# RWKV-5 attention into a mixture of four experts: bf16 transposes of scaled keys, a state update without its own keys, and a new order of the start

## The chip, the cores and the metric

One core of a Trainium2 chip runs the kernel. The metric is the device time of one execution in microseconds; less is better. Before the change three runs gave a median of 408.93 us (405.3 to 409.14).

## The reference

For each of 4 batches and 8 heads, attention walks over 768 positions with a state of 48 x 48; its result, 3072 rows of 384, goes through four experts, whose outputs are weighted per row and added.

```python
for t in range(S):
    cur = np.einsum('bhd,bhe->bhde', u[None] * kt, vt)
    y[:, :, t] = np.einsum('bhd,bhde->bhe', rt, state + cur)
    state = w[None, :, :, None] * state + np.einsum('bhd,bhe->bhde', kt, vt)
...
p = domain_probs / (domain_probs.sum(-1, keepdims=True) + 1e-09)
for e in range(E):
    h = np.maximum(x @ w1[e], 0.0)
    out += p[:, e:e + 1] * (h @ w2[e])
```

Shapes: r, k, v (4, 8, 768, 48), w and u (8, 48), w1 (4, 384, 1024), w2 (4, 1024, 384), all float32.

## The kernel before

The sequence is cut into 6 pieces of 128 positions. A chunk is one piece of one batch, all 8 heads; chunk ci is batch ci % 4, piece ci // 4, so there are 24, and four chunks in a row (a group) are one piece of all four batches. The state passes from chunk ci to ci + 4.

Attention of a chunk is a row of steps. `load` (L70 to L76) fetches R, K and V, 192 KB each, on SP's queue, into six buffers each. `pre` (L172 to L185) works on POOL: Vb (V in bf16), ruk = R * K * U, Kh (keys scaled for the state, in bf16, three buffers), dv; DVE reduces ruk to dcoef in between. `stR` and `stK` transpose R and K on PE in fp32, four transposes each for pairs of heads padded to 64, and DVE multiplies each result, 512 columns, with a table of decay powers into RsT and KsT. `stAt` makes the 8 products of keys and rows, masked by DVE into AtM. `stY` adds state and AtM products in psum, and DVE evicts them with dv into Ysb. `stS` makes the state matmuls St from Kh and Vb; POOL scales the old state by w^128 and DVE adds St. `stX` transposes Ysb, and DVE copies it to xTe. RT_ps, KT_ps and xT_ps share one psum buffer (tag tr), Y_ps and St_ps another (tag ys).

The experts: `l1` makes 128 rows of the hidden layer for all four chunks of a group (3 matmuls of 512 columns, evicted with Relu by ACT to hTs), `l2` the output of one chunk (8 matmuls of 384 columns), which DVE adds into oacc with the weight p_nat. Both use four psum buffers (tag mm).

The order on PE and POOL is that of the code; DVE, ACT and SP are ordered by the framework's scheduler, and every engine works in order. For the first four chunks attention steps and expert 0, chunk by chunk (L381 to L392), alternate. Then come 23 slots, one for each pair of expert and group from (expert 1, group 0) on. A slot is four times `l1`, `l1`, `l2` of the slot before; after each of these 12 parts a counter decides how many attention steps follow. Slots 0 and 1 take 12 steps each, the others 6:

```python
rate = 3 if si < 2 else 1.5
...
carry += rate / 3
while carry >= 1:
    carry -= 1
    f = next(steps, None)
```

The steps of a chunk stand in the order R(ci), Y(ci-1), K(ci), S(ci-1), At(ci), X(ci-1). Slot 3 is expert 0 of group 1 and needs xTe of chunk 7. From slot 18 on no attention is left.

Weights are cast to bf16 by DMAs on POOL's queue (`load_w1`, `load_w2`, 768 KB each): those of expert 0 at the start, the other six after attention steps 4, 9, 15 and 21 of the first four chunks (L374). At the start SP's queue also carries two DMAs of w (L83, single floats) and six of the weights p (L144, 16 bytes a piece).

Of the kernel before, what the change touches and what calls it, by code (L numbers as in the profile page):

```python
# [18 lines left out]
def kernel(  # L19
# [40 lines left out]


    RtB = [inputs.tile([128, H, P2], F32, name=f"Rt{i}") for i in range(NIN)]
    KtB = [inputs.tile([128, H, P2], F32, name=f"Kt{i}") for i in range(NIN)]
    KhB = [inputs.tile([128, H, P2], BF16, name=f"Kh{i}") for i in range(3)]
    for t in RtB + KtB + KhB:
        nc.vector.memset(t[:, :, D:P2], 0.0)

    Vts = {}

    def load(ci):  # L70
        b, c = ci % B, ci // B
# [75 lines left out]
    p_sum = consts.tile([128, TOTC, 1], F32)  # L147
    nc.vector.reduce_sum(p_sum, p_nat, axis=AX.X)
    nc.vector.tensor_scalar(p_sum, p_sum, scalar1=1e-9, scalar2=None, op0=ALU.add)
    p_rec = consts.tile([128, TOTC, 1], F32)  # L150
    nc.vector.reciprocal(p_rec, p_sum)
    nc.vector.tensor_mul(p_nat, p_nat, p_rec.to_broadcast((128, TOTC, E)))


    Sbd = [[inputs.tile([128, NP, 2 * D], BF16, name=f"S{b}_{i}") for i in range(2)]
           for b in range(B)]
    for b in range(B):
        for i in range(2):
            nc.gpsimd.memset(Sbd[b][i], 0.0)
# [160 lines left out]
    def att_steps(first, last):  # L320

        for ci in range(first, last + 1):
# [4 lines left out]
            if old:  # L327
                yield lambda ci=ci: stY(ci - 1)
# [98 lines left out]
```

## Time and profile before

| | us |
|---|---|
| median of three runs | 408.93 |
| the profiled execution | 405.69 |
| its span, first to last instruction | 403.6 |
| PE busy in the span | 326.0 |
| DVE, ACT, POOL busy | 168.0, 123.2, 124.7 |

The span is 2.1 us shorter than the profiled execution, which itself lies 0.8% below the median. Busy times of PE overlap and hold waiting inside a matmul, so stages are read by start times, not by sums of durations.

### The profile page before, as it was taken

To read this page: it belongs to the slowest core of one execution; us is meant where nothing else is said; L and a number is where in the kernel's file an instruction comes from. 1 tells how busy PE (TensorE), PEld (TensorE's weight loads), DVE (VectorE), ACT (ScalarE), POOL (GpSimd) and SP (SyncE) were. 2 spreads that over 40 slices of the span, in tenths; PEclk is the share of its full clock that TensorE was granted. 3 is DMA by queue.
4 is the path that set the end of the run, shared out by engine and by line. 5 is a ranking of instruction groups with operands and counts; after the bars stand their busy time and mean duration, and the time that the engine had idled before them with its cause. 6 is when DMAs were issued, how large, how long until landed. Compare 5 with 4: busy or idle time off the path is not lost.

```text
span 403.6 us, 5634 instructions
## 1 busy us (share of the span) xinstructions
PE 326.0 (81%) x2224; PEld 186.5 (46%) x2224; DVE 168.0 (42%) x328; ACT 123.2 (31%) x230; POOL 124.7 (31%) x176
## 2 busy tenths in 40 slices
PE   0156780868678979779798797799999999999996
PEld 0035650435444535445445454455555565555553
DVE  1057631554544443543435335436554444222223
ACT  1221330122133223233242232323333433444440
POOL 6148874753335044052251350531220000000000
PEclk9999997598999899998899898989999999999999
DMA  7999999972212322112321110110000100010002
GB/s 126 133 171 186 193 193 183 175 116 57 43 39 60 88 49 40 22 39 41 97 58 41 39 22 19 47 52 2 1 2 20 60 0 2 0 60 19 2 0 78
DMA packets 87993, 25.96 MB, mean 64 GB/s; under 512 B 79008, under 2 KB 86432, under 8 KB 87968
## 3 DMA queue, kind: packets, MB, share of 16 engines
q1 hardware_dynamic: 82208, 19.33, 26.5%
q0 software_dynamic: 5760, 6.29, 9.1%
q8 instruction: 17, 0.28, 0.3%
q14 instruction: 8, 0.07, 0.0%
HBM read 27.18 MB, written 4.72 MB: 79 GB/s over the span
## 4 chain that ended last, share of the span: by engine, by line
PE 50%; POOL 22%; DVE 10%; issue 8%; DMA 7%; SPq 1%; ACT 1%; POOLq 0%; ACTq 0%
PE out_ps L293 22%; PE hT_ps L280 20%; POOL ruk L180 5%; POOL ruk L179 5%; DMA Vt<-in_v_dram 4%; DVE AtM L218 4%; POOL Kh L182 4%; POOL S L259 3%; POOL dv L184 3%; PE RT_ps L191 3%; PE KT_ps L201 2%; DMA wT<-in_w_dram 2%; POOL Vb L178 2%; DVE oacc L300 2%; SPq L83 1%
## 5 line engine op out<-in xcount | busy, mean ns | idle before, releaser
L284 ACT ACTIVATE hTs<-hT_ps 128x512 bf16<-128x512 f32 (+1 forms) x216 | 116.5, 549 | 254.7 <-PE hT_ps L280 252.7
L280 PE MATMUL hT_ps<-xTe,w_sb 128*128 128x512 bf16 (+1 forms) x648 | 155.4, 372 | 0.0
L293 PE MATMUL out_ps<-w_sb,hTs 128*128 128x384 bf16 x768 | 147.3, 338 | 0.0
L293 PEld LDWEIGHTS <-hTs 128*128 128x128 bf16 x768 | 75.9, 100 | 54.7 <-issue 5.5
L280 PEld LDWEIGHTS <-w_sb 128*128 128x128 bf16 x648 | 59.1, 102 | 46.7 <-issue 5.8
L300 DVE SCALAR_TENSOR_TENSOR oacc<-out_ps,p_nat,oacc 128x384 f32<-128x384 f32 x72 | 44.4, 617 | 77.4 <-PE out_ps L293 77.3
L182 POOL TENSOR_TENSOR Kh<-Kt,W_sd 128x384 bf16<-128x384 f32 x20 | 20.0, 998 | 116.1 <-PE St_ps L250 114.0
L191 PE MATMUL RT_ps<-ident_f,Rt 128*128 128x128 f32 x96 | 17.7, 313 | 46.2 <-DVE xTe L268 33.5
L183 DVE TENSOR_REDUCE dcoef<-ruk 128x8 f32<-128x384 f32 x24 | 13.2, 551 | 65.3 <-POOL ruk L180 65.3
L191 PEld LDWEIGHTS RT_ps<-ident_f,Rt 128*128 128x128 f32 x96 | 11.8, 156 | 55.6 <-DVE xTe L268 42.3
L218 DVE TENSOR_TENSOR AtM<-At_ps,mask 128x512 bf16<-128x512 f32 x48 | 30.9, 683 | 3.6 <-PE At_ps L212 3.5
L184 POOL TENSOR_TENSOR dv<-Vt,dcoef 128x384 f32<-128x384 f32 x24 | 19.9, 830 | 35.0 <-DVE Ysb L240 28.7
L201 PE MATMUL KT_ps<-ident_f,Kt 128*128 128x128 f32 x96 | 16.6, 301 | 12.7 <-DVE RsT L195 12.6
L298 DVE TENSOR_SCALAR oacc<-out_ps,p_nat 128x384 f32<-128x384 f32 x24 | 14.8, 617 | 24.7 <-PE out_ps L293 24.7
L180 POOL TENSOR_TENSOR ruk<-ruk,U_sd 128x384 f32<-128x384 f32 x24 | 23.8, 994 | 1.9
L179 POOL TENSOR_TENSOR ruk<-Rt,Kt 128x384 f32<-128x384 f32 x24 | 24.0, 999 | 0.0
L195 DVE TENSOR_TENSOR RsT<-RT_ps,W1T 128x512 bf16<-128x512 f32 x24 | 16.6, 690 | 16.2 <-PE RT_ps L191 16.2
L178 POOL CAST Vb<-Vt 128x384 bf16<-128x384 f32 x24 | 12.1, 506 | 25.9 <-DMA Vt<-in_v_dram 18.7
L201 PEld LDWEIGHTS KT_ps<-ident_f,Kt 128*128 128x128 f32 x96 | 12.6, 153 | 15.7 <-DVE RsT L195 14.2
L240 DVE TENSOR_TENSOR Ysb<-Y_ps,dv 128x384 bf16<-128x384 f32 x24 | 13.3, 556 | 13.1 <-PE Y_ps L236 12.8
L236 PE MATMUL Y_ps<-Vb,AtM 128*128 128x48 bf16 x192 | 10.1, 193 | 10.4 <-POOL dv L184 9.6
L205 DVE TENSOR_TENSOR KsT<-KT_ps,W2T 128x512 bf16<-128x512 f32 x24 | 16.4, 684 | 3.6 <-PE KT_ps L201 3.6
(48 smaller groups left out, 128.7 us busy)
## 6 DMA issues: line engine op xcount, KB each, us to landing
w_sb<-in_moe_w_dram POOLq DMA_DIRECT2D x8, 768.0 KB, 12.9
Rt<-in_r_dram SPq DMA_DIRECT2D x24, 192.0 KB, 4.2
Kt<-in_k_dram SPq DMA_DIRECT2D x24, 192.0 KB, 3.9
Vt<-in_v_dram SPq DMA_DIRECT2D x24, 192.0 KB, 4.6
out_dram<-oacc SPq DMA_DIRECT2D x24, 192.0 KB, 1.8
logw_bc<-in_w_dram SPq DMA_DIRECT2D x1, 192.0 KB, 4.5
U_sd<-in_u_dram SPq DMA_DIRECT2D x1, 192.0 KB, 5.9
p_nat<-in_moe_domain_probs_dram SPq DMA_DIRECT2D x6, 8.0 KB, 2.2
```

The source lines that it names most:

```text
L178: nc.gpsimd.tensor_copy(Vb, Vt)
L179: nc.gpsimd.tensor_mul(ruk, Rt[:, :, 0:D], Kt[:, :, 0:D])
L180: nc.gpsimd.tensor_mul(ruk, ruk, U_sd)
L182: nc.gpsimd.tensor_mul(Kh[:, :, 0:D], Kt[:, :, 0:D], W3_sd)
L184: nc.gpsimd.tensor_mul(dv, Vt, dcoef.to_broadcast((128, H, D)))
L191: nc.tensor.transpose(ps[:, q, :], s["Rt"][:, 2 * q:2 * q + 2, :].rearrange("p a b -> p (a b)"), ident_f)
L201: nc.tensor.transpose(ps[:, q, :], s["Kt"][:, 2 * q:2 * q + 2, :].rearrange("p a b -> p (a b)"), ident_f)
L218: nc.vector.tensor_mul(s["AtM"][:, j], ps[:, j], mask[:, None, :].to_broadcast((128, NP, C)))
L280: nc.tensor.matmul(ps[:, 0:n, :].rearrange("p a b -> p (a b)"), w1_sb[:, e, db, fb * 128:(fb + 1) * 128], xTe[:, db, s0:s0 + n, :].rearran ...
L284: nc.scalar.activation(hTs[:, fb, s0:s0 + n, :], ps[:, 0:n, :], AF.Relu)
L293: nc.tensor.matmul(ps, hTs[:, fb, s, :], w2_sb[:, e, fb, :], start=(fb == 0), stop=(fb == NFB - 1))
L300: nc.vector.scalar_tensor_tensor(oaccs[ci], in0=ps, scalar=pe, in1=oaccs[ci], op0=ALU.mult, op1=ALU.add)
```

## The change

- R and K are scaled first, by DVE, with tables W1_sd (w^t) and W2_sd (w^-(t+1)), into one bf16 tile RK; four such tiles. `stRK` transposes both in bf16, 8 transposes into one psum tile of 1,024 columns, and ACT copies it to RKT. RsT, KsT and their two products go.
- Kh goes. The state matmuls take the keys in RK; DVE adds them to the old state into Tn, and POOL multiplies Tn with w^128 into the new state.
- The order of a chunk's steps is RK(ci), Y(ci-1), S(ci-1), At(ci), X(ci-1): five instead of six, 10 a slot in slots 0 and 1, then 5. `pre` runs one chunk ahead of its transposes (LEAD).
- In the start the four chunks run one after the other, each beside expert 0 of the chunk before (`fill`).
- w and p come as rows (wrow, prow) and are transposed by PE; w^128 is squared up on DVE; the two tables of powers cost two activations. Loads 0 and 1 stand ahead of these rows on SP's queue.
- The weights are issued after `pre` of chunks 0 and 2 to 7.

The core of the diff:

```diff
-    KhB = [inputs.tile([128, H, P2], BF16, name=f"Kh{i}") for i in range(3)]
...
-            nc.sync.dma_start(wT[j * P2:j * P2 + D, :],
-                              w.rearrange("(q j) d -> j d q", j=2)[j])
...
+    logw_bc = consts.tile([128, HD], F32)
+    nc.sync.dma_start(logw_bc, w.rearrange("h d -> (h d)")[None, :].to_broadcast((128, HD)))
+    load_w1(0)
+    load(0)
...
+    load(1)
+
+    wrow = consts.tile([NP, 2, P2], F32)
+    nc.vector.memset(wrow, 1.0)
+    nc.sync.dma_start(wrow[:, :, 0:D], w.rearrange("(q j) d -> q j d", j=2))
+    prow = consts.tile([TOTC, C, E], F32)
+    nc.sync.dma_start(prow, moe_domain_probs.rearrange("(n p) e -> n p e", p=C))
...
-    for c in range(NCH):
-        nc.sync.dma_start(
-            p_nat[:, c * B:(c + 1) * B, :],
-            moe_domain_probs.rearrange("(b c p) e -> c p b e", b=B, p=128)[c])
...
+    RKB = [consts.tile([128, 2, H, P2], BF16, name=f"RK{i}") for i in range(NRK)]
...
+        nc.tensor.transpose(ps, wrow.rearrange("q j d -> q (j d)"), ident_f[0:NP, 0:NP])
+        nc.vector.tensor_copy(wC, ps)
+        for _ in range(7):
+            nc.vector.tensor_mul(wC, wC, wC)
...
     def pre(ci):
+        nc.vector.tensor_mul(RK[:, 0, :, 0:D], Rt, W1_sd)
+        nc.vector.tensor_mul(RK[:, 1, :, 0:D], Kt, W2_sd)
...
-        nc.gpsimd.tensor_copy(Vb, Vt)
-        nc.gpsimd.tensor_mul(ruk, Rt[:, :, 0:D], Kt[:, :, 0:D])
-        nc.gpsimd.tensor_mul(ruk, ruk, U_sd)
-        if ci // B < NCH - 1:
-            nc.gpsimd.tensor_mul(Kh[:, :, 0:D], Kt[:, :, 0:D], W3_sd)
-        nc.vector.reduce_sum(dcoef, ruk, axis=AX.X)
+        nc.gpsimd.tensor_mul(ruk, Rt, Kt)
+        nc.gpsimd.tensor_mul(ruk, ruk, U_sd)
+        nc.vector.reduce_sum(dcoef, ruk, axis=AX.X)
+        nc.gpsimd.tensor_copy(Vb, Vt)
         nc.gpsimd.tensor_mul(dv, Vt, dcoef.to_broadcast((128, H, D)))
...
+    def stRK(ci):
         s = st[ci]
+        ps = psum.tile([128, 2, NP, C], BF16, tag="tr", bufs=1, name="RKT_ps")
+        for i in range(2):
+            for q in range(NP):
+                nc.tensor.transpose(ps[:, i, q, :],
+                                    s["RK"][:, i, 2 * q:2 * q + 2, :].rearrange("p a b -> p (a b)"),
+                                    ident)
+        s["RKT"] = work.tile([128, 2, NP, C], BF16, tag="RKT", bufs=3, name="RKT")
+        nc.scalar.copy(s["RKT"], ps)
...
-                             s["Kh"][:, 2 * q:2 * q + 2, :].rearrange("p a b -> p (a b)"),
+                             s["RK"][:, 1, 2 * q:2 * q + 2, :].rearrange("p a b -> p (a b)"),
...
-                nc.gpsimd.tensor_mul(S_new[pr, :, cl], S_now[pr, :, cl],
-                                     wC[pr, :, None].to_broadcast((P2, NP, D)))
-                nc.vector.tensor_add(S_new[pr, :, cl], S_new[pr, :, cl], ps[pr, :, cl])
+                nc.vector.tensor_add(Tn[pr], S_now[pr, :, cl], ps[pr, :, cl])
+                nc.gpsimd.tensor_mul(S_new[pr, :, cl], Tn[pr], wCb)
...
+    after = {0: [lambda: load_w2(0)], 2: [lambda: load_w1(1)], 3: [lambda: load_w2(1)],
+             4: [lambda: load_w1(2)], 5: [lambda: load_w2(2)],
+             6: [lambda: load_w1(3)], 7: [lambda: load_w2(3)]}
...
+                if new:
+                    yield lambda ci=ci: (pre_upto(ci + LEAD), stRK(ci))
+                if old:
+                    yield lambda ci=ci: stY(ci - 1)
+                    yield lambda ci=ci: stS(ci - 1)
+                if new:
+                    yield lambda ci=ci: stAt(ci)
+                if old:
+                    yield lambda ci=ci: stX(ci - 1)
...
+            per = (10 if si < 2 else 5) / 12
```

What the change moves on the engines, at two places.

POOL, before, around the state of chunk 8; the names are those of `pre` and `stS`:

```order
L259 TENSOR_TENSOR S_1_177<-S_0_176,wC 64x4x48 x2
L178 CAST Vb<-Vt 128x384
L179 TENSOR_TENSOR ruk<-Rt_77,Kt_83 128x384
L180 TENSOR_TENSOR ruk<-ruk,U_sd 128x384
L182 TENSOR_TENSOR Kh_86<-Kt_83,W_sd 128x8x48
L184 TENSOR_TENSOR dv<-Vt,dcoef 128x384
```

POOL, now, around the state of chunk 8:

```order
L247 TENSOR_TENSOR S_1_126<-Tn,wC 64x4x48 x2
L173 TENSOR_TENSOR ruk<-Rt,Kt 128x384
L174 TENSOR_TENSOR ruk<-ruk,U_sd 128x384
L176 CAST Vb<-Vt 128x384
L177 TENSOR_TENSOR dv<-Vt,dcoef 128x384
```

Kh is gone, ruk follows directly on the state, Vb has moved behind it, and the state reads Tn, which DVE writes.

DVE, before, in a slot of the middle; S is the sum of state and St_ps:

```order
L261 TENSOR_TENSOR S_0_182<-S_0_182,St_ps 64x4x48 x2
L300 SCALAR_TENSOR_TENSOR oacc<-out_ps,p_nat,oacc 128x384
L183 TENSOR_REDUCE dcoef<-ruk 128x8
L218 TENSOR_TENSOR AtM<-At_ps,mask 128x512 x2
L300 SCALAR_TENSOR_TENSOR oacc<-out_ps,p_nat,oacc 128x384
L268 COPY xTe<-xT_ps 128x3x128
L195 TENSOR_TENSOR RsT<-RT_ps,W1T 128x512
```

DVE, now, in a slot of the middle (the tiles RK_119 and RK_120 are two of the four RK tiles):

```order
L285 TENSOR_SCALAR oacc<-out_ps,p_nat 128x384
L246 TENSOR_TENSOR Tn<-S_1_130,St_ps 64x192 x2
L168 TENSOR_TENSOR RK_119<-Kt,W_sd 128x8x48
L175 TENSOR_REDUCE dcoef<-ruk 128x8
L287 SCALAR_TENSOR_TENSOR oacc<-out_ps,p_nat,oacc 128x384
L202 TENSOR_TENSOR AtM<-At_ps,mask 128x512 x2
L254 COPY xTe<-xT_ps 128x3x128
```

dcoef still stands ahead of AtM and xTe; an oacc now stands directly ahead of the addition to the state, and the product of K between that and dcoef.

DVE, now, ahead of the eviction of Y of chunk 4 (Ysb); RK_117 takes chunk 8 here, RK_118 chunk 9:

```order
L168 TENSOR_TENSOR RK_120<-Kt,W_sd 128x8x48
L167 TENSOR_TENSOR RK_117<-Rt,W_sd 128x8x48
L285 TENSOR_SCALAR oacc<-out_ps,p_nat 128x384
L202 TENSOR_TENSOR AtM<-At_ps,mask 128x512 x2
L167 TENSOR_TENSOR RK_118<-Rt,W_sd 128x8x48
L224 TENSOR_TENSOR Ysb<-Y_ps,dv 128x384
```

Before, dcoef of chunk 7 stood in this place, and no instruction of DVE read a load.

## Rows read from the trace of the kernel before

**Rows 1.** Windows: stretch, us, busy PE PEld DVE ACT POOL, PEclk, DMA share, GB/s.

```profile
0.00:53.80 53.80, 24.12 (x244) 19.20 (x245) 23.24 (x63) 13.48 (x46) 33.33 (x55) 1.00 1.14 163
53.80:122.10 68.30, 45.56 (x322) 25.78 (x320) 29.01 (x55) 14.32 (x24) 32.90 (x44) 0.85 0.67 110
122.10:270.00 147.90, 126.86 (x833) 69.92 (x831) 63.50 (x119) 43.63 (x74) 48.63 (x66) 0.92 0.21 48
270.00:342.50 72.50, 72.18 (x519) 41.16 (x518) 36.53 (x66) 27.89 (x47) 9.86 (x12) 1.00 0.04 13
342.50:403.60 61.10, 57.29 (x316) 30.46 (x313) 15.72 (x26) 23.84 (x40) 0.00 (x0) 0.99 0.07 26
```

**Rows 2.** Waits, whole span: who waited for whom, us, times, longest.

```profile
POOL Kh L182 <- PE St_ps L250: 114.0, 13, 11.2
...
DVE dcoef L183 <- POOL ruk L180: 65.3, 20, 10.8
...
PE RT_ps L191 <- DVE xTe L268: 33.5, 13, 3.7
```

**Rows 3.** Timeline, one chunk: start us, us, engine line op [idle before].

```profile
204.83 0.33 PE L250 MATMUL St_ps<-Vb,Kh 128*128 128x96 bf16 x4
...
205.20 0.71 DVE L261 TENSOR_TENSOR S<-S,St_ps 64x192 bf16<-64x192 bf16 x2 [0.69 <-PE St_ps L250]
...
206.99 1.08 POOL L259 TENSOR_TENSOR S<-S,wC 64x192 bf16<-64x192 bf16 x2
...
208.60 1.00 POOL L179 TENSOR_TENSOR ruk<-Rt,Kt 128x384 f32<-128x384 f32 x1
...
210.70 0.55 DVE L183 TENSOR_REDUCE dcoef<-ruk 128x8 f32<-128x384 f32 x1 [3.59 <-POOL ruk L180]
211.17 1.28 DVE L218 TENSOR_TENSOR AtM<-At_ps,mask 128x512 bf16<-128x512 f32 x2
212.37 0.61 DVE L298 TENSOR_SCALAR oacc<-out_ps,p_nat 128x384 f32<-128x384 f32 x1
212.89 0.35 DVE L268 COPY xTe<-xT_ps 128x384 bf16<-128x384 bf16 x1
...
213.30 0.66 PE L191 MATMUL RT_ps<-ident_f,Rt 128*128 128x128 f32 x4 [2.35 <-DVE xTe L268]
```

**Rows 4.** Timeline of PE, one chunk after 280 us.

```profile
282.43 0.33 PE L250 MATMUL St_ps<-Vb,Kh 128*128 128x96 bf16 x4
...
286.93 0.33 PE L267 MATMUL xT_ps<-ident,Ysb 128*128 128x128 bf16 x3
287.10 1.46 PE L280 MATMUL hT_ps<-xTe,w_sb 128*128 128x512 bf16 x6
288.64 0.66 PE L191 MATMUL RT_ps<-ident_f,Rt 128*128 128x128 f32 x4
289.14 1.46 PE L293 MATMUL out_ps<-w_sb,hTs 128*128 128x384 bf16 x8
...
293.40 0.60 PE L201 MATMUL KT_ps<-ident_f,Kt 128*128 128x128 f32 x4
293.84 1.46 PE L280 MATMUL hT_ps<-xTe,w_sb 128*128 128x512 bf16 x6
295.14 0.33 PE L250 MATMUL St_ps<-Vb,Kh 128*128 128x96 bf16 x4
```

**Rows 5.** DMA queues, 33 to 66 us: packets, MB, share of 16 engines.

```profile
q0 software_dynamic: 4320, 4.72, 83.7%
q1 hardware_dynamic: 8220, 1.55, 37.5%
```

**Rows 6.** DMA queues, 66 to 80 us.

```profile
q1 hardware_dynamic: 13011, 2.46, 117.7%
```

**Rows 7.** Timeline of PE: the state matmuls of chunk 4.

```profile
75.53 0.48 PE L250 MATMUL St_ps<-Vb,Kh 128*128 128x96 bf16 x4 [1.13 <-DVE Ysb L240]
```

**Rows 8.** Lines by form: the 512-column eviction on ACT.

```profile
L284 ACT ACTIVATE hTs<-hT_ps 128x512 bf16<-128x512 f32 x184 | 109.7, 597 | 231.2 <-PE hT_ps L280 229.6
```

More of the change, by code (lines that the diff above doesn't have):

```diff
@@ L148 @@
[L148 to L159, printed above, removed]
+    W1_sd = consts.tile([128, H, D], F32)
@@ L184, in pre @@
         nc.gpsimd.tensor_mul(dv, Vt, dcoef.to_broadcast((128, H, D)))
[L185 to L187 removed]
+        st[ci] = dict(RK=RK, Vb=Vb, dv=dv)
+    def stRK(ci):
         s = st[ci]
[L189 to L195 removed]
@@ L207, in stAt @@
+        for i in range(2):
+            for q in range(NP):
[4 more added lines that the diff above has]
+        nc.scalar.copy(s["RKT"], ps)
     def stAt(ci):
@@ L312, in load_next, with pre_upto @@
             state["loaded"] += 1
-    def pre_next():
-        if state["pre"] < TOTC:
+    def pre_upto(n):
+        while state["pre"] < min(n, TOTC):
             pre(state["pre"])
+            for f in after.get(state["pre"], []):
+                f()
             state["pre"] += 1
             load_next()
-    def att_steps(first, last):
-        for ci in range(first, last + 1):
-            new, old = ci < last, ci > first
-            if new:
-                pre_next()
-                yield lambda ci=ci: stR(ci)
-            if old:
-                yield lambda ci=ci: stY(ci - 1)
-            if new:
-                yield lambda ci=ci: stK(ci)
-            if old:
-                yield lambda ci=ci: stS(ci - 1)
-            if new:
-                yield lambda ci=ci: stAt(ci)
-            if old:
-                yield lambda ci=ci: stX(ci - 1)
@@ L338, with run @@
[L338 to L367 removed]
+    def run(gen):
+        f = next(gen, None)
+        if f:
+            f()
@@ new lines, with fill, att_steps @@
+    with tc.manual_schedule(engines={ET.PE, ET.Pool}):
+        load_next()
+        load_next()
+        def fill(ci):
+            for half in range(2):
+                yield lambda half=half: [l1(0, 0, fb, ci, 1) for fb in range(4 * half, 4 * half + 4)]
+            yield lambda: l2(0, 0, ci)
+        prev = iter(())
+        for ci in range(SUB):
+            pre_upto(ci + 1)
+            stRK(ci)
+            if ci == 0:
+                late_consts()
+            run(prev)
+            stAt(ci)
+            run(prev)
+            stY(ci)
+            run(prev)
+            stS(ci)
+            stX(ci)
+            prev = fill(ci)
+        run(prev)
+        run(prev)
+        def att_steps(first, last):
+            for ci in range(first, last + 1):
+                new, old = ci < last, ci > first
+                if new:
[7 more added lines that the diff above has]
+                    yield lambda ci=ci: stX(ci - 1)
@@ L381 @@
                     while carry >= 1:
                         carry -= 1
-                        f = next(steps, None)
-                        if f:
-                            f()
-                if prev:
-                    prev.pop(0)()
-                carry += rate / 3
-                while carry >= 1:
-                    carry -= 1
-                    f = next(steps, None)
-                    if f:
-                        f()
-            prev = [lambda e=e, sc=sc, s=s: l2(e, sc, s) for s in range(SUB)]
@@ L395 @@
-        for f in prev:
+                        run(steps)
+            l2s = [lambda e=e, sc=sc, s=s: l2(e, sc, s) for s in range(SUB)]
+        for f in l2s:
             f()
```

186 lines of the change are left out of this document (70 added, 116 removed).

## The prediction

> **What bounds the kernel now.** I read the windows by stretch first [rows 1]. The last 61.1 us hold no attention; PE works there almost without a gap. From 270 us on PE is busy 72.18 of 72.50 us although attention still runs. Between 122.1 and 270 it is busy 126.9 of 147.9 us at a clock of 0.92, and before 122.1 it is busy 69.7 us in all. So there are two losses: the start, and a stall in each of the slots of the middle. No engine but PE is close to full in any stretch.
>
> The list of waits tells what the stall is [rows 2]: PE's transposes of R wait for DVE's copy of xTe, DVE's reduction dcoef waits for POOL's ruk, and POOL's Kh waits for PE's state matmuls. The timeline of one chunk shows them as one chain [rows 3]. PE starts the state matmuls St at 204.83; POOL, which has run ahead until its three Kh buffers were full, now does Kh, dv, two S and Vb before it reaches ruk at 208.60; dcoef starts at 210.70. DVE works in order, so AtM, oacc and xTe stand behind dcoef, and PE, which needs the psum buffer that xTe empties, gets to RT at 213.30, after 2.35 us without work. The chain from St to RT takes 8.47 us. A chunk without this stall shows what PE itself needs [rows 4]: 12.71 us from St to St, 0.25 of it a small wait before RT (the six matmuls from 287.10 take 1.29, as the first of the next run from 293.84 do with 1.30), so 12.46 of work. Slots 3 to 17 lie between 122.1 and 342.5 us: 220.4 / 15 = 14.7 us each.
>
> In the start the DMA sets the pace. While weights were in flight their queue moved 4.72 MB in 33 us and the loads' queue only 1.55 MB (47 GB/s) [rows 5]; alone, from 66 to 80 us, the loads' queue moved 2.46 MB (176 GB/s) [rows 6].
>
> **The change part by part.**
>
> Transposes. Each chunk loses 8 fp32 transposes: RT holds PE 289.14 - 288.64 = 0.50 us, KT 0.44 [rows 4]. It gains 8 in bf16. The nearest row is xT: 3 bf16 transposes of the same size in 287.10 - 286.93 = 0.17, so 8 take 0.45. Ends: nothing gained (0.94), or 0.45; I take 0.45, since operation, type and size are the same. Work per chunk becomes 12.46 - 0.49 = 11.97 us.
>
> Evictions. The two DVE products RsT and KsT go; one ACT copy of 1,024 columns comes. No row shows it; it lies between one and two evictions of 512 columns, 0.60 to 1.19 us [rows 8], and I take 1.1. Two of PE's steps lie between the transposes and At, and ACT was busy only 43.6 of 147.9 us [rows 1], so it costs nothing; uncovered it would be 1.1 us a chunk.
>
> RK on DVE. Two products with both operands in SBUF come to DVE. Bounds: below dcoef's 0.55 for as many elements, or POOL's 1.00 for the same product [rows 3]; I take 0.55. Together with the products that go, DVE's load stays as it is (63.5 of 147.9 us). But these products read loads: the one for R of chunk 9 stands ahead of the eviction of Y of chunk 4 in DVE's order, and DVE waits there for that load. This matters in the start.
>
> The chain. Kh and its wait go. POOL now multiplies the state after DVE's Tn, and goes straight on to ruk. From St: 0.37 to Tn; first add 0.36; two S 1.08; two ruk 2.10; dcoef to its successor 0.47; oacc 0.52; AtM 1.20; xTe 0.41 until PE may go [rows 3]. Sum 6.51, and 0.36 more because an oacc now stands directly ahead of Tn: 6.9 us. PE's own work from St to the next transposes was 288.64 - 282.43 - 0.25 = 5.96; the new rate of 5 steps a slot puts one more pair of l1 groups in it, 1.30 [rows 4], so 7.26. The chain is 0.4 us shorter than its cover. Bounds: no stall, or, if DVE's RK product and POOL's ones hold each other up, 0.55 longer, hence 0.15 plus the error of the sum. I take 0.2 us for each of the 11 slots from 3 to 13 that still have a state update: 2.2 us. If the cover is gone, RK is late next, and behind it on PE the whole l2 and l1 stream.
>
> One rule of the Trainium skill speaks against this edit: the page "SBUF — State Buffer", section "Who interferes with whom", says that a VectorE instruction with two SBUF inputs contends with a GpSimd instruction that reads SBUF, as an exclusive lock. No row here has such a pair. By it the product of K, which stands between Tn and dcoef, would hold POOL's S or ruk for up to its length; that result is the second rival below.
>
> The start. The 8 small DMAs of w and p that held SP's queue become two row loads behind loads 0 and 1; DMA then runs from about 2.5 us. DVE can evict Y of chunk 4 when R of chunk 9 is there: the two tables, nine loads of three and one R, 30 x 0.197 = 5.9 MB on the loads' queue. Six weights are issued by then in POOL's new order; they take 33 us and leave 1.55 MB to the loads [rows 5]; the other 4.35 MB at 176 GB/s take 24.7 [rows 6]: 60 us. With a seventh weight in front, 5.5 us more and 0.26 MB less to do, 64. I take 63, and 64 for the state matmuls of chunk 4, against 75.5 before [rows 7]. From there to slot 3 before needed 122.1 - 75.5 = 46.6. Now three chunks go at the pace of the chain, 6.5 plus transposes, l1, Y and its eviction, some 9 us each, and then a slot of 12: 39, with 0.5 for the lower clock that the windows show in this stretch [rows 1]. Slot 3 starts at 64 + 39.5 = 103.5.
>
> Sum: 103.5 + 15 x 11.97 = 179.6, less 4 x 0.17 for the chunks without state matmuls, plus 2.2, plus the unchanged tail 61.1 = 345.7 us of span. The profiled execution took 405.69 for a span of 403.6, so 2.1 lie outside: 347.8, say 348. The median shown is 408.93, 0.8% above that execution.
>
> The late constants (7 squarings on DVE, 5 small transposes) lie in the first 25 us where loads are awaited; uncovered they are 2 to 3 us. Chunks of expert 0 that follow attention by one chunk fill PE while it waits there, no more.
>
> **The rivals.**
>
> 1. The loads are not the bound of the start. For it: two queues that held SP are gone, and weights are now spread over chunks 2 to 7. Against: the bytes are the same, and the DMA share of the first 53.8 us was 1.14 [rows 1]. Then the chain of 9 us a chunk from the first chunks on would put slot 3 near 88: 333 us.
>
> 2. The stall stays, smaller: RK on DVE and POOL's products exclude each other, or the chain has a piece I don't see. For it: a margin of 0.4 us in 7. Against: DVE's two-operand work is 1.1 us of 12. With 0.55 to 1.0 us a slot, and the clock dips that stalls of the middle brought (0.92 there against 1.00 without stalls [rows 1], about 1 us a slot): 11 x 2 = 22 more, 370 us.
>
> 3. The start gains nothing, since DVE waits for two loads more than before ahead of Y of chunk 4. For it: the order. Against: with SP free, R of chunk 9 comes earlier than chunk 7 was ready before. Slot 3 at 122: 367 us.
>
> 4. Slower than before: PE stays at its lower clock level (1.2 instead of 2.4 GHz) in slots with attention, as it did after the idle time in the start (0.85 in that stretch [rows 1]). Each such slot costs 12 us more. From five of the 15 slots on the change loses (58 / 12 = 4.8); with eight it takes 444 us. Against: from 270 on, attention with waits of 0.25 us left the clock at 1.00.
>
> **How the numbers follow.** The forecast has 0.62, rival 1 0.12, rival 2 0.15, rival 3 0.07, rival 4 0.04. The likeliest case alone spans 336 to 360: the start 8 us either way, the stall between nothing and 0.5 us a slot, the transposes at worst 0.5 us a chunk dearer. The range takes in rivals 1 to 3: 328 to 374; outside it lie the slow rival and the ends of the others. A measurement of this kernel tells about 1% from no change. All cases but rival 4 are faster by far more: faster 0.96, same 0.01, slower 0.03.
>
> **What would show it.** Right: PE's waits for xTe before the transposes add up to under 5 us instead of 33.5; slots 3 to 17 take about 12 us each at a clock near 1.00; the eight transposes take about 0.45 us; slot 3 starts near 103; DVE's RK products wait for loads in the first 65 us. Wrong: PE still waits over 0.5 us a chunk for xTe; POOL's ruk takes clearly more than 1.0 us beside RK; slot 3 starts before 95 or after 112; or the clock stays low past 120 us.

## The result and the profile after

Four runs of the changed kernel gave a median of 348.86 us (347.83 to 350.93), four of the kernel before 409.03: the ratio is 0.8543, with a 95% interval from 0.8467 to 0.8618. The forecast was 348 us. The profiled execution took 350.93 us for a span of 348.9.

The first view is that of the windows [rows 1], cut at the state matmuls of chunk 4, at the start of slot 3, at the last state update and at the start of slot 18 (columns: stretch, us, busy time and instructions of PE, PEld, DVE, ACT and POOL, PEclk, DMA share, GB/s).

```profile
0.00:65.80 65.80, 31.40 (x304) 22.96 (x306) 40.56 (x85) 18.93 (x47) 32.19 (x44) 0.87 1.03 182
65.80:106.70 40.90, 32.56 (x262) 18.63 (x267) 21.75 (x43) 15.78 (x24) 18.80 (x25) 0.92 0.65 119
106.70:239.20 132.50, 131.55 (x987) 74.47 (x1003) 72.56 (x142) 62.82 (x99) 49.31 (x66) 1.00 0.21 50
239.20:288.00 48.80, 46.84 (x342) 26.27 (x348) 20.44 (x38) 21.89 (x35) 7.70 (x10) 1.00 0.05 17
288.00:349.00 61.00, 56.96 (x310) 30.38 (x312) 15.70 (x26) 23.84 (x40) 0.00 (x0) 0.99 0.07 26
```

Slot 3 starts at 106.8 us, where it was 122.1, and slots 3 to 17 take 181.2 us instead of 220.4, at a clock of 1.00. From 106.7 to 239.2 PE is busy 131.55 of 132.50 us. The tail is as before. The start gives 15.3 us of the 54.7 by which the span is shorter, the slots 39.2.

The list of waits for the whole span [rows 2] (us in all, times, the longest):

```profile
POOL S L247 <- DVE Tn L246: 110.3, 16, 11.6
...
DVE dcoef L175 <- POOL ruk L174: 48.9, 20, 5.7
...
PE RKT_ps L185 <- DVE xTe L254: 14.3, 7, 3.6
...
PE p_ps L151 <- DVE p_e L147: 5.7, 1, 5.7
```

PE's wait for xTe falls from 33.5 to 14.3 us. By the timeline 12.7 us of it lie in the start, ahead of the transposes of chunks 1 to 3 and 6 to 8, and 1.6 in slot 14. In that slot the scheduler put the dcoef of the next chunk, too, between AtM and xTe: at 247.25 us DVE had waited 1.12 us there for ruk. The first wait shown moved with the change: POOL, which had waited for St in order to write Kh, now waits 110 us for Tn, which also comes from St. So POOL still starts its work for the next chunk only when St is done.

The timeline of one slot, which answers to [rows 3] and [rows 4] (start, duration, engine, line, operation, idle time before):

```profile
118.63 0.33 PE L235 MATMUL St_ps<-Vb,RK 128*128 128x96 bf16 x4
...
119.37 0.72 DVE L246 TENSOR_TENSOR Tn<-S,St_ps 64x192 f32<-64x192 bf16 x2
...
119.78 1.29 POOL L247 TENSOR_TENSOR S<-Tn,wC 64x192 bf16<-64x192 f32 x2 [7.11 <-DVE Tn L246]
...
120.12 0.58 DVE L168 TENSOR_TENSOR RK<-Kt,W_sd 128x384 bf16<-128x384 f32 x1
121.15 1.00 POOL L173 TENSOR_TENSOR ruk<-Rt,Kt 128x384 f32<-128x384 f32 x1
...
122.22 0.99 POOL L174 TENSOR_TENSOR ruk<-ruk,U_sd 128x384 f32<-128x384 f32 x1
...
123.25 0.55 DVE L175 TENSOR_REDUCE dcoef<-ruk 128x8 f32<-128x384 f32 x1 [2.55 <-POOL ruk L174]
...
123.84 0.62 DVE L285 TENSOR_SCALAR oacc<-out_ps,p_nat 128x384 f32<-128x384 f32 x1
...
124.37 1.28 DVE L202 TENSOR_TENSOR AtM<-At_ps,mask 128x512 bf16<-128x512 f32 x2
...
124.60 1.46 PE L266 MATMUL hT_ps<-xTe,w_sb 128*128 128x512 bf16 x5
...
125.57 0.35 DVE L254 COPY xTe<-xT_ps 128x384 bf16<-128x384 bf16 x1
...
125.97 0.61 PE L185 MATMUL RKT_ps<-ident,RK 128*128 128x128 bf16 x8
...
130.68 0.33 PE L235 MATMUL St_ps<-Vb,RK 128*128 128x96 bf16 x4
```

St at 118.63 sets off Tn, S, ruk, dcoef, AtM, xTe, and the transposes follow at 125.97: 7.34 us, where the chain had taken 8.47. The six l1 matmuls from 124.60 (the record lacks one) hold PE for 1.30 us like any other six, so PE's own work ended 0.07 us before. PE waits for next to nothing, but the chain has no margin either. From St to St it is 12.05 us.

The start, by PE's timeline: the state matmuls of chunks 4 to 8 (L235) and the transposes that waited for xTe (L185). The first row answers to [rows 7].

```profile
65.83 0.33 PE L235 MATMUL St_ps<-Vb,RK 128*128 128x96 bf16 x4 [0.73 <-DVE Ysb L224]
...
72.29 1.01 PE L185 MATMUL RKT_ps<-ident,RK 128*128 128x128 bf16 x8 [3.58 <-DVE xTe L254]
...
75.87 0.48 PE L235 MATMUL St_ps<-Vb,RK 128*128 128x96 bf16 x4 [0.65 <-DVE Ysb L224]
...
83.00 0.61 PE L185 MATMUL RKT_ps<-ident,RK 128*128 128x128 bf16 x8 [1.94 <-DVE xTe L254]
...
85.77 0.33 PE L235 MATMUL St_ps<-Vb,RK 128*128 128x96 bf16 x4
...
91.79 0.61 PE L185 MATMUL RKT_ps<-ident,RK 128*128 128x128 bf16 x8 [1.84 <-DVE xTe L254]
...
106.59 0.33 PE L235 MATMUL St_ps<-Vb,RK 128*128 128x96 bf16 x4
```

The groups of the page for the new operations; the ACT copy answers to [rows 8], POOL's product S stands here because its mean was 502 ns before:

```profile
L247 POOL TENSOR_TENSOR S<-Tn,wC 64x192 bf16<-64x192 f32 x32 | 19.4, 605 | 111.5 <-DVE Tn L246 110.3
L189 ACT COPY RKT<-RKT_ps 128x1024 bf16<-128x1024 bf16 x24 | 24.3, 1012 | 45.6 <-PE RKT_ps L185 45.6
...
L167 DVE TENSOR_TENSOR RK<-Rt,W_sd 128x384 bf16<-128x384 f32 x24 | 16.1, 673 | 14.5 <-DMA Rt<-in_r_dram 6.1
```

### The profile page after: what moved, and what is told of

It reads as the page before. It is cut to its first block, busy times and chain, and to the rows that moved or that the text cites. A ratio compares the mean times of both kernels' runs of the same rounds, so it can differ in the third digit from the quotient of the medians.

```text
span 348.9 us, 5568 instructions
## 1 busy us (share of the span) xinstructions
PE 299.3 (86%) x2193; PEld 172.7 (50%) x2229; DVE 171.0 (49%) x333; ACT 143.3 (41%) x245; POOL 108.0 (31%) x145
## 4 chain that ended last, share of the span: by engine, by line
PE 74%; POOL 11%; DVE 6%; issue 5%; SPq 3%; DMA 1%; POOLq 0%; DVEq 0%
PE out_ps L279 34%; PE hT_ps L266 32%; PE RKT_ps L185 3%; POOL ruk L174 3%; POOL ruk L173 3%; SPq L80 2%; PE At_ps L196 2%; POOL dv L177 1%; POOL S L247 1%; PE Y_ps L220 1%; DVE AtM L202 1%; PE Y_ps L213 1%; POOL Vb L176 1%; PE St_ps L235 1%; SPq L88 1%
## 5 line engine op out<-in xcount | busy, mean ns | idle before, releaser
L266 PE MATMUL hT_ps<-xTe,w_sb 128*128 128x512 bf16 (+1 forms) x612 | 145.6, 366 | 3.3 <-DVE xTe L254 1.4
L279 PE MATMUL out_ps<-w_sb,hTs 128*128 128x384 bf16 x768 | 141.1, 328 | 0.0
L279 PEld LDWEIGHTS <-hTs 128*128 128x128 bf16 x768 | 73.5, 98 | 50.9 <-issue 1.0
L247 POOL TENSOR_TENSOR S<-Tn,wC 64x192 bf16<-64x192 f32 x32 | 19.4, 605 | 111.5 <-DVE Tn L246 110.3
L189 ACT COPY RKT<-RKT_ps 128x1024 bf16<-128x1024 bf16 x24 | 24.3, 1012 | 45.6 <-PE RKT_ps L185 45.6
L185 PE MATMUL RKT_ps<-ident,RK 128*128 128x128 bf16 x192 | 16.8, 237 | 28.5 <-DVE xTe L254 14.3
L185 PEld LDWEIGHTS <-RK 128*128 128x128 bf16 x192 | 14.2, 106 | 35.5 <-issue 18.3
L167 DVE TENSOR_TENSOR RK<-Rt,W_sd 128x384 bf16<-128x384 f32 x24 | 16.1, 673 | 14.5 <-DMA Rt<-in_r_dram 6.1
L168 DVE TENSOR_TENSOR RK<-Kt,W_sd 128x384 bf16<-128x384 f32 x24 | 15.4, 643 | 0.6
L246 DVE TENSOR_TENSOR Tn<-S,St_ps 64x192 f32<-64x192 bf16 x32 | 11.1, 347 | 1.5 <-PE St_ps L235 1.0
```

The source lines that it names most:

```text
L185: nc.tensor.transpose(ps[:, i, q, :], s["RK"][:, i, 2 * q:2 * q + 2, :].rearrange("p a b -> p (a b)"), ident)
L189: nc.scalar.copy(s["RKT"], ps)
L247: nc.gpsimd.tensor_mul(S_new[pr, :, cl], Tn[pr], wCb)
L266: nc.tensor.matmul(ps[:, 0:n, :].rearrange("p a b -> p (a b)"), w1_sb[:, e, db, fb * 128:(fb + 1) * 128], xTe[:, db, s0:s0 + n, :].rearran ...
L279: nc.tensor.matmul(ps, hTs[:, fb, s, :], w2_sb[:, e, fb, :], start=(fb == 0), stop=(fb == NFB - 1))
```

## The experiments

The ratios below are to the kernel before, measured beside each experiment. The yardstick is the changed kernel run again in experiment 9: 0.8556 (0.8521 to 0.8591). A difference of 0.01 is 4.1 us.

### The chain from St to the next transposes

**Experiment 1: one more POOL product in the chain.** In `pre`, ahead of ruk:

```diff
+        if ci // B < NCH - 1:
+            Kx = work.tile([128, H, D], BF16, tag="Kx", bufs=2, name="Kx")
+            nc.gpsimd.tensor_mul(Kx, Kt, W2_sd)
         nc.gpsimd.tensor_mul(ruk, Rt, Kt)
```

> The changed kernel with one more POOL product per chunk (keys times W2_sd into a bf16 tile that nobody reads, chunks 0 to 19), placed directly ahead of ruk; nothing is left out. Theory A, the chain: from the state matmuls St of a chunk over Tn, S, ruk, dcoef, AtM and xTe to the next transposes takes 7.34 us in the changed kernel, PE's own work there 7.26 to 7.33, so no margin is left; the product (1.00 us and 0.07 until the next) lengthens the chain by 1.07 in each of the 11 slots with a state update (11.8 us) and in the 4 chunks between 60 and 107 us (4.3 us): 349 + 16 = 365 us, slots 3 to 13 of 13.1 instead of 12.04 us, PE waits for xTe of about 1 us in each. Theory B, PE alone: POOL is busy 31% of the span and PE is full, so the product is hidden: 347 to 351 us.

Measured: 359.74 us, ratio 0.8773 (0.8729 to 0.8816). Its timeline, one slot:

```profile
132.25 0.33 PE L238 MATMUL St_ps<-Vb,RK 128*128 128x96 bf16 x4
...
134.76 1.00 POOL L175 TENSOR_TENSOR Kx<-Kt,W_sd 128x384 bf16<-128x384 f32 x1
...
139.07 1.45 PE L269 MATMUL hT_ps<-xTe,w_sb 128*128 128x512 bf16 x6 [0.69 <-DVE oacc L290]
...
145.24 0.33 PE L238 MATMUL St_ps<-Vb,RK 128*128 128x96 bf16 x4
```

The product at 134.76 moves ruk and dcoef, and the slot takes 12.99 us instead of 12.05: 0.94 more for 1.00 of added work, the same in slots 3 to 11. (The last two slots with a state update take 12.03 us as ever: POOL runs ahead, and the chunks from 20 on, which it prepares there, have no such product.) POOL is busy a third of the time, and its work still costs nearly its full length. That is theory A. Part of the wait now lies elsewhere: PE waits 0.69 us for oacc, which stands behind dcoef on DVE and has to empty a psum buffer of the expert matmuls. From St of chunk 4 to St of chunk 8 it took only 1.6 us more, and 9 slots, not 11, are longer, so the total stays under the 365 us expected.

**Experiment 2: dcoef one step group later.** `pre` is split; from slot 0 on dcoef and dv of a chunk are issued behind stX:

```diff
-        nc.vector.reduce_sum(dcoef, ruk, axis=AX.X)
...
+        def rest():
+            nc.vector.reduce_sum(dcoef, ruk, axis=AX.X)
+            nc.gpsimd.tensor_mul(dv, Vt, dcoef.to_broadcast((128, H, D)))
...
-                    yield lambda ci=ci: stX(ci - 1)
+                    yield lambda ci=ci: (stX(ci - 1), flush())
```

> The changed kernel with dcoef and dv of a chunk issued one step group later (from slot 0 on): POOL makes ruk of a chunk ahead of the state product S of the chunk two before it, so ruk is a slot old when DVE comes to dcoef. Theory A, the chain with POOL in it sets slots 0 to 13: without POOL's 3.5 us between Tn and dcoef it is about 4.7 us long (0.74 to Tn, 0.72, RK 0.58, dcoef 0.5, oacc 0.53, AtM 1.2, xTe 0.4), PE's waits for xTe in slots 0 and 1 go (3.6, 1.9 and 1.8 us) and the ones of about 0.1 in slots 3 to 13: 349 - 7.4 - 1 = 341 us, St of chunk 8 at 99 to 100 us instead of 106.6. Theory B, DVE's own order or the loads set slots 0 and 1, not POOL: 346 to 350 us.

Measured: 357.88 us, ratio 0.8737 (0.8703 to 0.8770), so neither: slower than the changed kernel by 0.018.

```profile
129.68 0.33 PE L247 MATMUL St_ps<-Vb,RK 128*128 128x96 bf16 x4
...
132.19 0.83 POOL L185 TENSOR_TENSOR dv<-Vt,dcoef 128x384 f32<-128x384 f32 x1
...
135.09 0.55 DVE L184 TENSOR_REDUCE dcoef<-ruk 128x8 f32<-128x384 f32 x1 [3.34 <-POOL ruk L179]
...
142.51 0.33 PE L247 MATMUL St_ps<-Vb,RK 128*128 128x96 bf16 x4
```

The scheduler, which orders DVE, put dcoef where it had been, between Tn and AtM, and there it waits for a ruk that POOL makes only now; the edit had merely put dv (0.83 us at 132.19) in front of it. The chain grew by that, and so did the slot: 12.83 us, 0.78 more. The expectation failed because it took DVE's order for that of the code. As a measurement it repeats the first experiment with another operation.

**Experiment 8: DVE's order set by hand.** The block of the slots gets its own context, in which DVE too follows the code:

```diff
+    with tc.manual_schedule(engines={ET.PE, ET.Pool, ET.DVE}):
         slots = [(e, sc) for sc in range(NSC) for e in range(E)][1:]
```

> The changed kernel with DVE's order in the slots that of the code instead of the scheduler's: dcoef of a chunk then stands behind xTe, not ahead of AtM and xTe; nothing is left out. In the second experiment the chain grew by as much as POOL was given in it (0.79 us, dv), so the order of DVE still had dcoef in the chain. Theory A: with POOL out of the chain from St to the next transposes (Tn 1.46, then AtM behind At, 4.5, xTe 5.0, some 5.3 us in all against PE's 7.26) PE never waits for xTe in slots 3 to 13, slots of 11.95 us instead of 12.04, and slots 0 and 1 lose their waits of 3.6, 1.9 and 1.8 us, St of chunk 8 comes about 37 us behind St of chunk 4 instead of 40.8: 339 to 344 us. Theory B: another wait takes its place (Ysb behind dcoef, or the loads): 346 to 352 us.

Measured: 336.30 us, ratio 0.8274 (0.8189 to 0.8360).

```profile
105.25 0.33 PE L235 MATMUL St_ps<-Vb,RK 128*128 128x96 bf16 x4
...
106.40 1.08 POOL L247 TENSOR_TENSOR S<-Tn,wC 64x192 bf16<-64x192 f32 x2 [4.03 <-DVE Tn L246]
...
108.75 1.28 DVE L202 TENSOR_TENSOR AtM<-At_ps,mask 128x512 bf16<-128x512 f32 x2
...
110.11 0.36 DVE L254 COPY xTe<-xT_ps 128x384 bf16<-128x384 bf16 x1
...
112.51 0.61 PE L185 MATMUL RKT_ps<-ident,RK 128*128 128x128 bf16 x8
...
112.88 0.55 DVE L175 TENSOR_REDUCE dcoef<-ruk 128x8 f32<-128x384 f32 x1
...
117.22 0.33 PE L235 MATMUL St_ps<-Vb,RK 128*128 128x96 bf16 x4
```

dcoef now stands at 112.88, behind xTe (110.11) and RK, and waits for nothing. xTe is done 2 us before PE wants its transposes. A slot takes 11.97 us, just the work that the prediction had counted, and from St of chunk 4 to that of chunk 8 (60.53 to 93.27 us) it is 32.7 instead of 40.8. The edit moves other work of DVE as well, RK above all. But in the changed kernel DVE stood idle for 2.55 us behind RK until ruk came (123.25 in the slot shown there), so it is this wait for ruk, ahead of AtM and xTe, that went. POOL's piece of the chain had cost the changed kernel 8 us in slots 0 to 2, 0.07 in each of slots 3 to 13, and 1.6 in slot 14.

**Experiment 7: the kernel before without Kh on POOL.** The middle alone, from the other side:

```diff
-            nc.gpsimd.tensor_mul(Kh[:, :, 0:D], Kt[:, :, 0:D], W3_sd)
+            nc.scalar.copy(Kh[:, :, 0:D], Kt[:, :, 0:D])
```

> The kernel before with Kh made by ACT as a plain copy of K instead of by POOL as a product with the decay table (the factor is left out of the state update, so this part of the computation is changed; POOL loses 1.00 us a chunk and its wait for a free Kh buffer). Theory A: Kh and its wait on POOL are what makes the chain from St to the next R transposes 8.47 us long, 2.35 longer than PE's work beside it: without them the stall falls by 1.0 to 2.35 us in each of the 15 slots, and part of the clock comes back (up to 8 us in the stretch from 122 to 270): 375 to 395 us. Theory B, another piece sets the stall (POOL then waits for another buffer just as long, or ACT's copy holds up the evictions): 403 to 412 us.

Measured: 380.01 us, ratio 0.9340 (0.9248 to 0.9432). The wait of PE (compare [rows 2]):

```profile
PE RT_ps L191 <- DVE xTe L268: 9.0, 8, 3.4
```

PE's wait for xTe falls from 33.5 to 9.0 us, and slots 3 to 17 (130.3 to 317.8 us in this trace) take 187.5 instead of 220.4: 33 us less, at a clock of 1.00. The start loses 8 us (slot 3 at 130.3 instead of 122.1): there PE waited once 15.9 us for an eviction of ACT. So theory A holds for the middle: POOL's Kh made the stall, and with it the lower clock. POOL still waits, now for Ysb in order to write dv (104.9 us in all), and PE's waits show little of it.

### The transposes

**Experiment 6: the transposes twice.**

```diff
-        for i in range(2):
+        for i in (0, 1, 0, 1):
             for q in range(NP):
                 nc.tensor.transpose(ps[:, i, q, :],
```

> The changed kernel with the 8 bf16 transposes of R and K made twice (16 per chunk, the second time over the same psum; results unchanged). 8 take 0.44 us in its trace; 16 would take 0.88, near the 0.94 that the fp32 transposes of the kernel before took. Theory A: these transposes stand on PE's path in every slot, behind the wait: 0.44 us more in each of slots 3 to 17 (6.6 us) and in most of the 9 chunks of the start (2 to 4 us): 357 to 360 us, slots of 12.48 us. Theory B, a stall elsewhere in the slot absorbs them: 347 to 351 us.

Measured: 357.38 us, ratio 0.8785 (0.8695 to 0.8875), slots of 12.49 us: 0.44 us more in each. The eight transposes cost PE their full time, and replacing eight fp32 ones (0.94 in [rows 4]) by eight in bf16 saves about 0.5 us a slot.

### The start

**Experiment 9: the changed kernel again,** without an edit.

> The changed kernel again, word for word, as the yardstick for the experiments on the start and to see how far its first 60 us repeat. In its first profile DVE waited 1.8 and 4.2 us for the loads of R of chunks 5 and 6, which the other profiles of the same start did not all show. Theory A: those waits are chance of that execution; St of chunk 4 lies between 59 and 66 us from execution to execution, everything from there on repeats within 1 us: 346 to 351 us, slots of 12.04 us. Theory B: the waits belong to the kernel and come again at 35 and 43 us: 349 to 351 us.

Measured: 350.02 us (347.00 to 351.79). The profile, with a span of 345.0, has no wait of DVE for R of chunks 5 and 6; those waits come in some executions and not in others. It does have the wait that the prediction spoke of, for R of chunk 9 ahead of the eviction of Y of chunk 4 (first fence). The first profile has it too, though its row names PE (second fence): there the DMA of R of chunk 9 was issued at 49.78 us and landed 14.9 us later, at 64.68, and RK started at 64.75.

```profile
61.06 0.56 DVE L167 TENSOR_TENSOR RK<-Rt,W_sd 128x384 bf16<-128x384 f32 x1 [0.95 <-DMA Rt<-in_r_dram]
...
62.14 0.33 PE L235 MATMUL St_ps<-Vb,RK 128*128 128x96 bf16 x4 [1.70 <-DVE Ysb L224]
```

```profile
49.78 2.98 SPq L80 DMA_DIRECT2D Rt<-in_r_dram  x1
...
64.75 0.56 DVE L167 TENSOR_TENSOR RK<-Rt,W_sd 128x384 bf16<-128x384 f32 x1 [0.34 <-PE hT_ps L266]
```

The wait is 0.95 us at 61.06 here, with St of chunk 4 at 62.14, and 0.34 us in the first profile, with St at 65.83. So R of chunk 9 was the last to come in both, by less than 1 us. Slot 3 starts at 102.9 in this execution, at 106.8 in the first. That one also had the lower clock: 0.50 from 40 to 50 us, after a stretch in which PE was busy 4.96 of 10 us.

**Experiment 3: without four of the eight weights.**

```diff
-             4: [lambda: load_w1(2)], 5: [lambda: load_w2(2)],
-             6: [lambda: load_w1(3)], 7: [lambda: load_w2(3)]}
+             }
...
-                             w1_sb[:, e, db, fb * 128:(fb + 1) * 128],
+                             w1_sb[:, e % 2, db, fb * 128:(fb + 1) * 128],
```

and the same in `l2`.

> The changed kernel without the loads of w1 and w2 of experts 2 and 3 (3.1 MB of DMA writes to the core less in the first 80 us); these experts compute with the weights of experts 0 and 1, so part of the computation is changed. Theory A, as the prediction has it: Y of chunk 4 waits for the load of R of chunk 9, which stands behind the weights; with four weights less in front, R of chunk 9 is there some 12 to 16 us earlier, and the start ends that much earlier: 333 to 338 us. Theory B, from the trace of the changed kernel: the only long waits for loads are those for R of chunks 5 and 6 (at 35.6 and 43.0 us), ahead of the weights of experts 2 and 3 (issued from 44.8 us on); behind them the chain of DVE and POOL sets the pace, so St of chunk 4 stays at 64 to 66 us: 346 to 349 us.

Measured: 344.73 us, ratio 0.8418 (0.8395 to 0.8441): 0.0138 or 5.6 us less than the yardstick. St of chunk 4 came at 58.73, and DVE waited for no load after 26 us. Between the theories, nearer to B: the loads hold the start by 3 to 7 us (58.7 against 62.1 and 65.8), and right below them lies another bound, the chain of the first four chunks (25.3, 34.0, 42.6, 49.1, 58.7 us for St of chunks 0 to 4).

**Experiment 5: the eight small DMAs put back.**

```diff
     load(0)
...
+        for j in range(2):
+            nc.sync.dma_start(wT[j * P2:j * P2 + D, :],
+                              w.rearrange("(q j) d -> j d q", j=2)[j])
...
+    for c in range(NCH):
+        nc.sync.dma_start(
+            p_x[:, c * B:(c + 1) * B, :],
+            moe_domain_probs.rearrange("(b c p) e -> c p b e", b=B, p=128)[c])
```

> The changed kernel with the eight small DMAs of w and p of the kernel before put back on SP's queue behind load 0 (into tiles that nobody reads; the row loads stay). In the kernel before they held that queue for 6.97 + 8.78 us. Theory A, SP's queue matters in the start as the prediction has it: every load from U and load 1 on comes up to 15.7 us later, and at least what the DMA engines can't make good: St of chunk 4 at 70 to 80 us instead of 62 to 66, 357 to 364 us. Theory B, bytes and the chain of the chunks set the start, and the queue has room: 347 to 351 us.

Measured: 357.61 us, ratio 0.8790 (0.8717 to 0.8864). St of chunk 0 at 32.35 instead of 25.6, of chunk 4 at 71.86: 0.023 or 9.6 us, as theory A has it. The rows of w and p are worth that much. What the other parts of the new start (the order of `fill`, the weights issued later than before) are worth, no run shows.

**Experiment 4: the p part of the late constants later; experiment 10: this and DVE's order of experiment 8 together.** All lines of `late_consts` from p_sum on become `late_p`:

```diff
             stX(ci)
+            if ci == 0:
+                late_p()
             prev = fill(ci)
```

> The changed kernel with the p part of the late constants (sum, reciprocal, p_e, four transposes, p_nat) issued behind xT of chunk 0 instead of ahead of its At; PE no longer waits 5.7 us for p_e ahead of At of chunk 0. Theory A, the loads of R of chunks 5 and 6 set the pace of chunks 1 and 2: chunk 0 comes up to 5 us earlier, AtM of chunk 2 still waits for R of chunk 6 until 43 us, and the time stays: 347 to 350 us. Theory B, the constants are on the path of the start: 343 to 345 us.

> The changed kernel with two edits: DVE's order in the slots that of the code, and the p part of the late constants behind xT of chunk 0. Theory A, with the chain of the slots out of the way the chunks of the start are the bound, and the 2.6 to 2.9 us by which St of chunk 0 came earlier in the fourth experiment stay until the end: 332 to 335 us. Theory B, the loads bind from 40 to 60 us (DMA queues are full until 75 us): St of chunk 4 stays at 60 us: 335 to 338 us.

Measured: 346.61 us, ratio 0.8476 (0.8428 to 0.8525), and together 332.90, ratio 0.8134 (0.8113 to 0.8154). St of chunk 0 came at 22.7 instead of 25.6. The first is 0.008 or 3 us below the yardstick, with intervals that just touch; the second 3.4 us below DVE's order alone, which was measured at another time, with intervals that lie apart. In the profiles less is left: St of chunk 8 came 1.9 us earlier in the first (100.87 against 102.73) and 0.8 in the second (92.43 against 93.27). So the constants cost between 1 and 3 us. The second kernel is the fastest kernel of this study: 0.8134 / 0.8556 = 0.951 of the changed one.

**Experiments 11 and 12: w1 of expert 0 behind chunk 0, or all other weights later,** each on top of experiment 10:

```diff
-    load_w1(0)
     load(0)
...
-    after = {0: [lambda: load_w2(0)], 2: [lambda: load_w1(1)], 3: [lambda: load_w2(1)],
+    after = {0: [lambda: load_w1(0), lambda: load_w2(0)], 2: [lambda: load_w1(1)], 3: [lambda: load_w2(1)],
```

```diff
-    after = {0: [lambda: load_w2(0)], 2: [lambda: load_w1(1)], 3: [lambda: load_w2(1)],
-             4: [lambda: load_w1(2)], 5: [lambda: load_w2(2)],
-             6: [lambda: load_w1(3)], 7: [lambda: load_w2(3)]}
+    after = {1: [lambda: load_w2(0)], 3: [lambda: load_w1(1)], 4: [lambda: load_w2(1)],
+             6: [lambda: load_w1(2)], 7: [lambda: load_w2(2)],
+             8: [lambda: load_w1(3)], 9: [lambda: load_w2(3)]}
```

> As the experiment before, and w1 of expert 0 is issued behind pre of chunk 0 (with w2 of expert 0) instead of ahead of load 0. K of chunk 0 landed at 10.8 us beside w1. Theory A, the start is a chain from the first K on: K of chunk 0 comes 3 to 5 us earlier, St of chunk 0 at 18 to 20 us instead of 22.7, and the end as much earlier: 328 to 332 us. Theory B, the bytes bind: the same bytes have to come until R of chunk 9, or w1 arrives too late for expert 0 of chunk 0, and the gain is lost by St of chunk 4: 332 to 336 us.

> The kernel of the tenth experiment with every weight behind w1 of expert 0 issued one or two chunks later (after pre of chunks 1, 3, 4, 6, 7, 8 and 9 instead of 0 and 2 to 7); bytes and order are the same, only the loads of R, K and V get more of the DMA queues before 60 us. Theory A, the loads up to R of chunk 9 hold the start by the 3 to 5 us that St of chunk 4 gained when four weights were left out: St of chunk 4 at 55 to 57 us instead of 59.7, 328 to 331 us. Theory B, what is left of the start is the chain of its four chunks (8.4 us each, 9.8 to 10.3 for the last), and loads have only a small share: St of chunk 4 at 58 to 60 us, 331 to 334 us, or later where a weight now comes too late for its expert.

Measured: 334.79 us, ratio 0.8179 (0.8159 to 0.8199), and 340.10, ratio 0.8300 (0.8260 to 0.8340). Both are misses for theory A. In the first St of chunk 0 came at 17.8, but that of chunk 1 only at 33.4, as before (33.0). DVE waited 1.2 and 0.7 us for R and K of chunk 3 ahead of AtM of chunk 1, and ahead of the eviction of Y of chunk 1 stood the product RK for R of chunk 4:

```profile
27.57 5.28 DVE L168 TENSOR_TENSOR RK<-Rt,W_sd 128x384 bf16<-128x384 f32 x1
```

It took 5.28 us instead of 0.55, beside POOL, which went from one instruction to the next without a gap in that time. PE waited 3.8 us for the eviction. In experiment 10 the same product took 2.57. So part of the gain was lost to this product and not to late loads. In the second PE waited for weights:

```profile
PE out_ps L281 <- DMA w_sb<-in_moe_w_dram: 2.9, 1, 2.9
...
PE hT_ps L268 <- DMA w_sb<-in_moe_w_dram: 1.8, 1, 1.8
```

So weights issued this much later come too late, and the first move shows no more than that the gain of chunk 0 does not last. Neither tests R of chunk 9 again: with DVE's order set by hand the last RK ahead of the eviction of Y of chunk 4 is that of chunk 6.

## Why the prediction was right

The forecast of 348 us came out to within the scatter of the runs. The mechanism was right in the main, the stall and the start's last load; part of the closeness is luck, where errors cancelled. The steps, one by one:

- **The stall and its cause** [rows 2, 3]: right, and shown from both sides. A POOL product put into the chain of the changed kernel brings the stall back (experiment 1), and without Kh on POOL the kernel before loses 33 of the 39 us that slots 3 to 17 lost in the change; the rest, 6.3, fits the transposes: about 0.5 us for each of the 15 slots is 7.5, of which the wait in slot 14 takes back 1.6.
- **Work per chunk**, 11.97 us: a slot without waits took 11.97 in the eighth experiment. Eight bf16 transposes took 0.44 us (0.45 forecast), the ACT copy 1.01 (1.1), hidden.
- **The chain**, "0.4 us shorter than its cover": this step failed, though the 0.2 us of stall taken from it did no harm. It is 7.34 us, not 6.9, and no shorter than its cover. The terms that were too small are mainly two: the S products, with 1.37 from the first to ruk instead of 1.08 (0.21 of it since RK runs on DVE beside them, 0.08 the step to ruk, which the sum left out), and dcoef, with 0.59 to its successor instead of 0.47. The stall was about 0.07 us a slot; by the first two experiments what is added beyond that counts nearly in full (0.94 of 1.00 and 0.78 of 0.83).
- **RK on DVE**, 0.55 us each: that is right for an undisturbed one; the means are 0.67 and 0.64. The bound for the case that DVE and POOL hold each other up, 0.55 more, was too small: in the start of the changed kernel one took 1.87 us.
- **The start**: St of chunk 4 was forecast at 64 us and came at 65.8 and 62.1; slot 3 at 103.5 and came at 106.8 and 102.9. R of chunk 9, forecast for 63, landed at 64.7 and 60.9. The pace of 9 us was near (10.0, 9.9 and 8.8 in the first profile, then 12.0). But this load is only just the last to come, by 0.3 and 0.95 us; in the first profile waits for R of chunks 5 and 6 and the lower clock had made the chain late as well. The sum had one bound where there are two: without the last weights the chain alone came 3 to 7 us earlier. That both executions fell so near 64 is partly luck.
- **The late constants**, "lie in the first 25 us where loads are awaited": wrong by what the fourth and tenth experiments point to. PE waited 5.7 us for p_e, and 1 to 3 us of this reached the end, about the price given for the uncovered case (2 to 3).
- **Slots 3 to 17 and the tail**: 181.2 us against 181.1 in the sum (179.6 - 0.7 + 2.2), tail 60.9 against 61.1. This closeness is luck: the 11 slots with a state update took 132.5, 1.4 less than the sum has for them (11 x 11.97 + 2.2), and the other four, with the wait in slot 14 that the sum does not have, 1.5 more.
- **The sign** "waits for xTe under 5 us" failed: 14.3. It counted slots 3 to 17 only. It left out the first chunks (5.4 us, ahead of the transposes of chunks 1 to 3) and the chain in slots 0 and 1 (7.4 us), whose 9 us a chunk the prediction itself had worked out as longer than PE's work.

Of the rivals, the first (start not bound by loads, slot 3 at 88) fell: with four weights left out slot 3 still started at 100.8, and the 93.4 of the eighth experiment came with all loads in place, from the cut in the chain. The second was there in kind, as below, but at 0.2 us a slot it took half of the margin of 0.4 and no more. The third and fourth did not happen: slot 3 came 15 us earlier, and the clock in the slots was 1.00.

## What to carry to other kernels

An engine that is busy a third of the time can still set the pace when its work lies on a chain that starts and ends at the busy engine: compare the chain's length with the work beside it, and expect what is added to cost nearly its full length once the two are equal (0.94 us of 1.00 here). When such a chain is cut, look at the order of every engine on it, above all where a scheduler sets it: here one reduction in front of a copy, on an engine half idle, was worth 3% after all the rest had been done. And the start, bound by loads, had a second bound close by here; a sum should look for both.

## What the hardware showed that was not expected

In these traces a DVE product of two operands in SBUF and POOL's work lengthen each other. From the eighth experiment:

```profile
63.94 0.99 POOL L174 TENSOR_TENSOR ruk<-ruk,U_sd 128x384 f32<-128x384 f32 x1
63.99 1.36 DVE L167 TENSOR_TENSOR RK<-Rt,W_sd 128x384 bf16<-128x384 f32 x1
...
64.88 0.83 POOL L176 CAST Vb<-Vt 128x384 bf16<-128x384 f32 x1
...
65.28 0.85 DVE L168 TENSOR_TENSOR RK<-Kt,W_sd 128x384 bf16<-128x384 f32 x1
```

RK takes 1.36 us beside ruk, which keeps its 0.99; the next RK takes 0.85 beside Vb, which takes 0.83. Without such a partner they take 0.55 (at 111.95) and 0.51 (at 109.57, beside AtM, which reads psum) in the same trace. In the changed kernel S has RK beside it in each slot and takes 605 ns on average; in the eighth experiment RK has moved away and S takes 504. The Trainium skill, "SBUF — State Buffer", section "Who interferes with whom", tells of an exclusive lock between such instructions. The rows agree that the two hold each other up: RK beside ruk lost 0.81 us of ruk's 0.99, as a lock would have it, while in the second pair the loss is shared, 0.30 and 0.32. The price goes by the company: in the slots of the changed kernel it was only 0.2 us a chunk, but in the eleventh experiment one RK lost 4.7 us (5.28 instead of 0.55) beside POOL instructions that followed each other without a gap.
